# Attention and MLP on one core: tokens mapped 112 by 4, two heads scored as half-array matmuls, fixed buffers, a list-scheduled order

## The chip, the cores and the metric

One of the eight cores of a Trainium2 chip. The metric is device microseconds of one execution.

In the views, PE is TensorE, PEld its weight loads, DVE VectorE, ACT ScalarE, POOL GpSimd, and SP the queue that issues most of the DMA transfers.

## The reference

```python
# q, k, v: (8 batches, 12 heads, 448 tokens, 64); w_in: (768, 2048); w_out: (2048, 768); float32
q_n, k_n = rmsnorm(q, g_q), rmsnorm(k, g_k)          # over the 64 of a head
attn = softmax(q_n @ k_n.T / sqrt(64))               # per batch and head
x = (attn @ v) -> (8 * 448 tokens, 12 * 64 = 768)
h = x @ w_in
out = (h * clip(h + 3, 0, 6) / 6) @ w_out            # (3584, 768)
```

## The kernel before

It works on 48 head pairs (8 batches of 6). A pair's q and k are squared, reduced and scaled (normalisation), transposed on TensorE, multiplied to scores, exponentiated by ACT, and multiplied with v; a column of ones beside v gives the softmax sum. Matmuls of the MLP (`h` of the batch before, `y` of the batch before that) are merged between the attention steps by a fixed proportion. 448 tokens are 3 tiles of 128 and a rest of 64. The rests of two heads share one tile, which needs loads, squares, masks and transposes of its own.

A head has only 64 dimensions, and TensorE contracts 128 rows. The two heads of a pair lie above one another in the 128 rows, and a copy of k for each head is masked with zeros for the other head:

```python
kp = kp_pool.tile([128, 2, SM], BF16, name="kp")
for a in range(2):                       # masked copy of k for each head
    nc.vector.tensor_scalar_mul(kp[:, a, :], ps[:, 1]..., gmask[:, a:a + 1])
...
def score(P, u):                         # u = 0..6: 3 tiles x 2 heads, and the rest
    ...
    ps = ps_S.tile([128, S], FP32, name="s_ps")
    nc.tensor.matmul(out=ps[:], lhsT=lhsT, rhs=st["qT", b][:, j, :], start=True, stop=True)
    nc.scalar.activation(out=st["e", P][:, u, :], in_=ps[:], func=EXP, bias=zero_c[:], scale=1.0)
...
def att_items(P):                        # the order: loads 5 pairs ahead, prep 3, transposes 2
    items = [(0.0, lambda: load_step(P + 5)), (0.0, lambda: prep_step(P + 3)),
             (0.36, lambda: trans_step(P + 2))]
    ...
```

## Time and profile before

581.9 us (two runs, 581.15 and 582.66). Four parts of the profile's page follow: busy time of each engine; the span in 40 slices of 14.6 us, in tenths of busy time, with the granted TensorE clock; the chain of work that ended last; and two groups of instructions (busy us, mean ns of one, then idle time before them and who ended it).

```profile
PE 469.9 (81%) x3848; PEld 278.2 (48%) x3848; DVE 245.7 (42%) x544; ACT 320.5 (55%) x638; POOL 212.9 (37%) x245
...
PE   0045859877689888888788899888899999999996
...
PEclk9997998998999999979998999989999999999999
...
PE 35%; POOL 23%; DMA 19%; DVE 10%; ACT 5%; issue 4%; SPq 4%; POOLq 0%; ACTq 0%
DMA qk<-in_k_dram 15%; PE h_ps L356 14%; PE y_ps L373 13%; POOL qks L165 9%; POOL sq L138 9%; DVE ssq L159 4%; ACT t_sb L361 3%; PE s_ps L270 3%; SPq L190 2%; PE t_ps L248 2%; SPq L145 2%; POOL sqr L138 1%; DMA vr<-in_v_dram 1%; DMA qkr<-in_k_dram 1%; DVE xn L298 1%
...
L271 ACT ACTIVATE eT<-s_ps,zero_c 128x448 bf16<-128x448 f32 x336 | 200.9, 643 | 52.5 <-PE s_ps L270 50.0
...
L138 POOL TENSOR_TENSOR sq<-qk 128x768 f32<-128x768 f32 x45 | 66.0, 1468 | 88.4 <-DMA qk<-in_k_dram 80.6
```

TensorE is the busiest engine, but its slices are full only in the last third of the span. Nothing runs on it in the first two slices, and then they read between 4 and 9. The chain says why: it runs only 35% through TensorE, and 38% through the k loads (15%) and POOL (23%, most of it squaring and scaling), that is, through the preparation of the pairs.

Busy time overstates matmuls, because they overlap: one of 448 columns is listed with 360 ns, but the next starts 189 ns after it. For a sum one needs the time from one start to the next in back-to-back stretches, which I took from the trace: 448 columns 189 ns, 384 columns 162 ns, 512 columns 215 ns, 128 columns 56 ns. The next view is the timeline (start us, duration us, what, count, and in brackets the idle time before) of the first pair.

```profile
13.18 0.84 ACT L136 ACTIVATE sq<-qk 128x768 f32<-128x768 f32 x1 [8.63 <-DMA qk<-in_q_dram]
...
15.88 13.13 SPq L190 DMA_DIRECT2D vr<-in_v_dram  x4
32.71 0.84 ACT L136 ACTIVATE sqr<-qkr 128x768 f32<-128x768 f32 x1 [17.30 <-DMA vr<-in_v_dram]
...
34.72 0.50 PE L248 MATMUL t_ps<-identity,qks 128*128 128x128 bf16 x3 [34.72 <-POOL qks L165]
...
39.30 0.91 PE L270 MATMUL s_ps<-qT,kp 128*128 128x448 bf16 x2 [0.45 <-DVE qT L233]
```

The first pair's square is done at 14 us, but its transpose starts at 34.72 and its score at 39.30. In between, the second square of the rest tokens stands in ACT's queue ahead of everything else and waits until 32.71 for loads of small pieces.

| from the trace of before | us |
|---|---|
| span | 582.8 |
| until the first matmul | 34.7 |
| matmuls at their full-clock pace | 425.4 |
| extra while the clock was half | 13.1 |
| TensorE waiting: before 45 us, 45 to 100, after 100 | 5.2, 19.5, 80.1 |
| after the last matmul | 4.6 |

### The profile page before, as it was taken

How to read it: one execution, taken by the hardware profiler on the slowest of the kernel's cores; microseconds unless marked ns; L12 is line 12 of the kernel's file. 1: busy time of each engine (PE TensorE's matmuls, PEld its weight loads, DVE VectorE, ACT ScalarE, POOL GpSimd, SP SyncE). 2: the span in 40 equal slices, each digit the busy share in tenths (PEclk: the TensorE clock that was granted, in tenths of full speed). 3: DMA queues.
4: the chain of work that ended last, by engine and by line, in shares of the span. 5: the costliest groups of instructions: out<-in, count | busy, mean ns of one | idle time of the engine just before them, and what ended most of it. 6: DMA issues, size and time to landing. Idle time of an engine off the chain costs nothing.

```text
span 582.8 us, 9889 instructions
## 1 busy us (share of the span) xinstructions
PE 469.9 (81%) x3848; PEld 278.2 (48%) x3848; DVE 245.7 (42%) x544; ACT 320.5 (55%) x638; POOL 212.9 (37%) x245
## 2 busy tenths in 40 slices
PE   0045859877689888888788899888899999999996
PEld 0023535543345555544444455555455566654454
DVE  0035658864544453435543443544443434232200
ACT  1055977865566655636555666555667665733221
POOL 5069769974543532324434353223221100000000
PEclk9997998998999999979998999989999999999999
DMA  8974995462134222212222123222110000010012
GB/s 204 231 149 120 201 236 162 132 154 82 55 86 132 82 70 72 93 54 55 62 77 80 56 82 96 73 64 70 55 55 29 29 28 28 28 42 27 28 56 68
DMA packets 69648, 50.98 MB, mean 87 GB/s; under 512 B 22753, under 2 KB 68833, under 8 KB 69601
## 3 DMA queue, kind: packets, MB, share of 16 engines
q1 hardware_dynamic: 63168, 43.27, 26.4%
q0 software_dynamic: 2976, 6.29, 5.8%
q10 hardware_dynamic: 3456, 0.79, 0.7%
q8 instruction: 30, 0.49, 0.3%
q14 instruction: 18, 0.14, 0.1%
HBM read 45.61 MB, written 11.01 MB: 97 GB/s over the span
## 4 chain that ended last, share of the span: by engine, by line
PE 35%; POOL 23%; DMA 19%; DVE 10%; ACT 5%; issue 4%; SPq 4%; POOLq 0%; ACTq 0%
DMA qk<-in_k_dram 15%; PE h_ps L356 14%; PE y_ps L373 13%; POOL qks L165 9%; POOL sq L138 9%; DVE ssq L159 4%; ACT t_sb L361 3%; PE s_ps L270 3%; SPq L190 2%; PE t_ps L248 2%; SPq L145 2%; POOL sqr L138 1%; DMA vr<-in_v_dram 1%; DMA qkr<-in_k_dram 1%; DVE xn L298 1%
## 5 line engine op out<-in xcount | busy, mean ns | idle before, releaser
L271 ACT ACTIVATE eT<-s_ps,zero_c 128x448 bf16<-128x448 f32 x336 | 200.9, 643 | 52.5 <-PE s_ps L270 50.0
L361 ACT ACTIVATE t_sb<-h_ps,half_c 128x384 f32<-128x384 f32 (+1 forms) x128 | 81.1, 634 | 78.2 <-PE h_ps L356 78.0
L356 PEld LDWEIGHTS <-w_in_sb 128*128 128x128 bf16 x768 | 72.5, 98 | 95.5 <-issue 54.9
L165 POOL TENSOR_TENSOR qks<-qk,rs 128x384 bf16<-128x384 f32 x96 | 77.7, 831 | 103.4 <-PE t_ps L248 71.1
L270 PE MATMUL s_ps<-qT,kp 128*128 128x448 bf16 x288 | 97.1, 360 | 2.5 <-DVE kp L254 1.3
L138 POOL TENSOR_TENSOR sq<-qk 128x768 f32<-128x768 f32 x45 | 66.0, 1468 | 88.4 <-DMA qk<-in_k_dram 80.6
L159 DVE TENSOR_REDUCE ssq<-sq 128x12 f32<-128x768 f32 x48 | 45.7, 952 | 95.7 <-POOL sq L138 87.3
L279 PEld LDWEIGHTS <-eT 128*128 128x128 bf16 x1152 | 66.3, 100 | 30.4 <-issue 2.5
L248 PE MATMUL t_ps<-identity,qks 128*128 128x128 bf16 x288 | 26.1, 228 | 44.6 <-POOL qks L165 41.1
L379 ACT COPY y_sb<-y_ps 128x384 f32<-128x384 f32 x56 | 26.8, 479 | 44.0 <-PE y_ps L373 43.9
L248 PEld LDWEIGHTS <-qks 128*128 128x128 bf16 x288 | 20.9, 101 | 54.1 <-POOL qks L165 41.9
L130 ACT ACTIVATE rs<-ssq,eps_c 128x12 f32<-128x12 f32 x48 | 15.0, 313 | 51.9 <-POOL qks L165 37.3
L356 PE MATMUL h_ps<-xT_984,w_in_sb 128*128 128x512 bf16 x96 | 26.6, 394 | 11.3 <-DVE gT_1641 L363 10.7
L270 PEld LDWEIGHTS <-kp 128*128 128x128 bf16 x288 | 27.9, 99 | 16.3 <-DVE kp L254 1.7
L254 DVE TENSOR_SCALAR kp<-t_ps,gmask 128x384 bf16<-128x384 bf16 x96 | 35.2, 409 | 0.0
L356 PE MATMUL h_ps<-xT_2580,w_in_sb 128*128 128x512 bf16 x96 | 26.5, 389 | 6.9 <-DVE gT_3374 L363 6.7
L373 PE MATMUL y_ps<-w_out_sb,gT_1641 128*128 128x384 bf16 x128 | 28.0, 338 | 1.7 <-ACT y_sb L379 1.6
L373 PE MATMUL y_ps<-w_out_sb,gT_3374 128*128 128x384 bf16 x128 | 27.3, 332 | 1.7 <-ACT y_sb L379 1.6
L356 PE MATMUL h_ps<-xT_1757,w_in_sb 128*128 128x384 bf16 x96 | 22.0, 337 | 7.9 <-DVE gT_2459 L363 7.8
L250 DVE COPY qT<-t_ps 128x384 bf16<-128x384 bf16 x48 | 17.0, 355 | 26.6 <-PE t_ps L248 26.4
L298 DVE TENSOR_TENSOR xn<-x_ps,rd 128x384 bf16<-128x384 f32 x48 | 26.7, 555 | 1.2
L336 PE MATMUL xt_ps<-identity,xn 128*128 128x128 bf16 x144 | 17.3, 226 | 12.1 <-DVE xn L298 11.8
(104 smaller groups left out, 745.5 us busy)
## 6 DMA issues: line engine op xcount, KB each, us to landing
qk<-in_q_dram SPq DMA_DIRECT2D x48, 192.0 KB, 2.5
qk<-in_k_dram SPq DMA_DIRECT2D x48, 192.0 KB, 2.8
vf<-in_v_dram SPq DMA_DIRECT2D x48, 192.0 KB, 2.5
out_dram<-y_sb SPq DMA_DIRECT2D x48, 192.0 KB, 1.9
w_in_sb<-in_moe_w_in_dram POOLq DMA_DIRECT2D x6, 512.0 KB, 11.9
w_out_sb<-in_moe_w_out_dram POOLq DMA_DIRECT2D x4, 768.0 KB, 14.2
vr<-in_v_dram SPq DMA_DIRECT2D x16, 96.0 KB, 6.4
out_dram<-y_sb SPq DMA_DIRECT2D x16, 96.0 KB, 2.2
```

Source lines behind the costliest of these rows:

```text
L138: nc.gpsimd.tensor_tensor(out=out, in0=x, in1=x, op=A_MULT)
L159: nc.vector.tensor_reduce(out=ssq[:], in_=sq[:].rearrange("p (n d) -> p n d", d=D), axis=AX_X, op=A_ADD)
L165: nc.gpsimd.tensor_tensor(out=qks[:, i].rearrange("p t h d -> p h t d"), in0=qk[:, i].rearrange("p h (t d) -> p h t d", d=D), in1=rs4[:, i ...
L248: nc.tensor.transpose(ps[:, i, t, :], qks[:, i, t].rearrange("p h d -> p (h d)"), identity[:])
L254: nc.vector.tensor_scalar_mul(kp[:, a, :], ps[:, 1].rearrange("p t c -> p (t c)"), gmask[:, a:a + 1])
L270: nc.tensor.matmul(out=ps[:], lhsT=lhsT, rhs=st["qT", b][:, j, :], start=True, stop=True)
L271: nc.scalar.activation(out=st["e", P][:, u, :], in_=ps[:], func=EXP, bias=zero_c[:], scale=1.0)
L279: nc.tensor.matmul(out=dst[:, a * E1:(a + 1) * E1], lhsT=eT[:, u, c0:c0 + 128], rhs=va[:, a, t, :], start=(first and a == 0 and t == 0), s ...
L298: nc.vector.tensor_tensor(out=xn[:], in0=xv[:, :, :, 0:D], in1=rd[:].unsqueeze(3).to_broadcast([128, NT, 2, D]), op=A_MULT)
L356: nc.tensor.matmul(out=h_ps[:, 0:n], lhsT=w_in_sb[:, kt, f * 128:(f + 1) * 128], rhs=st["xT", G][:, kt, :], start=(kt == 0), stop=(kt == N ...
L361: nc.scalar.activation(out=t_sb[:, 0:n], in_=h_ps[:, 0:n], func=RELU, bias=half_c[:], scale=1.0 / 6.0)
L373: nc.tensor.matmul(out=y_ps, lhsT=gT[:, f, i * 128:(i + 1) * 128], rhs=w_out_sb[:, f, nh * HALF:(nh + 1) * HALF], start=(f == 0), stop=(f ...
```

## The change

The intent: no rest tokens (448 = 4 tiles of 112), no masked copies (each head's scores contract 64 rows, one head in the upper and one in the lower half of the array, so that both matmuls can run at once), one `exp` over both heads, and an order found by a list schedule: before the kernel is built, a program simulates the engines with a fixed cost for each step and gives the engine that comes free next its most urgent ready step. The file is nearly rewritten; its core:

```diff
-    ps_S = pool("ps_S", 3, space=PSUM)                 # 3 score buffers, one bank each
+    S_r = [psum.tile([128, 2, 512], FP32, name=f"S{i}") for i in range(2)]  # 2, two banks each
@@ scores
-        ps = ps_S.tile([128, S], FP32, name="s_ps")
-        nc.tensor.matmul(out=ps[:], lhsT=lhsT, rhs=st["qT", b][:, j, :], start=True, stop=True)
-        nc.scalar.activation(out=st["e", P][:, u, :], in_=ps[:], func=EXP, bias=zero_c[:], ...)
+            for a in range(2):
+                r = slice(a * 64, a * 64 + 64)
+                em(nc.tensor.matmul(
+                    out=ps[:, a, 0:S], lhsT=kT[r, t * TP:t * TP + 128], rhs=qT[r, :],
+                    start=True, stop=True))
+            em(nc.scalar.activation(
+                out=eT[:, t], in_=ps[0:TP, :, 0:S], func=EXP, bias=0.0, scale=1.0))
+        plan.add(PE, 0.25, 0.42, want, f_s, ...)       # 0.25 us of TensorE in the schedule
@@ preparation
+        early = P < 3                                   # squares on ACT, else on POOL
+            eng = DVE if P == 0 or (P < 8 and i == 0) else POOL   # scaling of q, of k
@@ order
-        for _, fn in merge(att, mlp):
-            fn()
+    for i in plan.order():                              # greedy, over simulated engines
+        plan.ops[i][4]()
```

Matmuls per pair change from 7 transposes, 7 scores of 448 columns, 28 value products and 3.5 transposes back to 8, 8 (half array), 32 and 4. The MLP's columns are the same. `em` ties each instruction to the one before it on its engine, so the planned order is the executed order.

## The prediction

> **What bounds the kernel now.** TensorE. In back-to-back stretches of the timeline a 448-column matmul starts every 189 ns, 384 columns every 162, 512 every 215, 128 every 56, 65 every 33. With the counts of the groups view that is: scores 336 x 189 = 63.5 us, values 1152 x 33 + 192 x 56 = 49, transposes 504 x 56 = 28, h 145, y 145: 430 us of matmul work in a 583 us span. The remaining 150 us are: 34.7 us before the first transpose (timeline: the 256-byte rest-token loads hold the DMA queues, and the rest squares sit ahead of everything in order on ACT and POOL); about 113 us of stalls after it; 4.5 us of last copy and store. The windows view puts the stalls early: PE busy 0.68 at 40 to 60 us, about 0.8 from 130 to 300, 0.97 from 400 on. The chain of waits names loads of k (15%), POOL scaling and squares (18%): input preparation, not ACT (55% busy).
>
> **What the change does, costed.**
> 1. No rest tokens: their small loads (24 us of full-DMA time, summed packet times), squares, masks and transposes go. First transpose at 11 to 13 us: q and k land at about 8, then half square 0.6, reduction 0.7, two small ACTIVATEs 0.6, scaling 0.7. Gain about 23 us.
> 2. Scores: 4 pairs of K=64 matmuls instead of 7 of K=128 per head pair. The Trainium skill ("TensorE: Matmul & The Clock Gate", Packing small matmuls) says different row groups run concurrently, starts about 4 ns apart; "TensorEngine Tiling (Array Packing)", Key Properties, says that changing tiling mode drains the engine. No run here shows either. Estimate: 189 ns plus about 60 for two switches, 192 x 0.25 = 48 us against 63.5. If they ran serially: 73 us.
> 3. Values 1536 x 33 = 51, transposes 384 x 49 + 192 x 56 = 30, h 768 x 189 = 145, y 145: unchanged within 3 us. Total matmul work about 419 us.
> 4. ACT: 192 exps of 896 columns without bias pointer, about 0.91 us each (0.643 + 448 x 0.83 ns - 0.10, the difference of copy and relu at 384), 175 us against 201. Off the path, except during the first six pairs, where ACT at about 4 us per pair sets the pace and PE has only 2.6 us of work.
> 5. POOL about 4.7 us per pair (square 1.95, two scalings 1.1, cast 0.6), under the 8 to 9 us a pair takes: no limit. DVE about unchanged.
> 6. List order plus early loads: most of the preparation stalls go.
>
> **Sum.** First scores 12; pairs of batch 0 until about 36 (ACT-bound); batch 1 with h of batch 0 until about 71; then 370 us of matmul work; 4.5 tail: 446 at no stall. With 5% stalls (two PSUM buffers for h and y, one for values; h groups back to back need about 1.5 us against 1.13 of matmuls) and some half-clock windows: **468 us**, range 450 to 498. Faster by over 2%: 0.97; within: 0.02; slower: 0.01.
>
> **What would show it.** First PE work near 12 us; score matmuls of a pair starting within 10 ns and about 0.25 us to the next group; exp near 0.91 us; PE busy over 0.9 from 80 us on; chain dominated by PE h and y, POOL and k loads under 10% together; ACT about 290 us busy.
>
> **What would make it wrong.** Each tiling-mode switch draining fully (0.17 us each, twice per group: +50 us); serial halves (+25); the fixed order fitting the chip badly so that waits on the single value buffer, two score buffers or h evacuations cost over 10% (+25); weights landing late.

## The result

500.0 us (two runs, 499.02 and 500.98), ratio 0.8587, 95% interval 0.8534 to 0.8640. That is 2 us outside the range (450 to 498) and 32 us above the predicted 468. All ratios here are those of a kernel's runs to the runs of the kernel before in the same rounds, so not quite the ratio of the medians quoted. The same lines of the page, after:

```profile
PE 461.8 (93%) x4160; PEld 264.9 (53%) x4160; DVE 234.5 (47%) x432; ACT 295.1 (59%) x485; POOL 213.6 (43%) x204
...
PE   1688999899998999899999999999999999989996
...
PEclk9999899999999999999999999999999999999999
...
PE 81%; DMA 7%; DVE 3%; ACT 3%; issue 2%; POOL 2%; SPq 1%; POOLq 0%; ACTq 0%; DVEq 0%
PE M L397 30%; PE M L364 26%; PE S L303 9%; PE X L320 9%; DMA qk<-in_k_dram 6%; PE S L283 3%; PE X L342 2%; ACT eT L308 2%; DMA qk<-in_q_dram 1%; DVE gT L375 1%; ACT ts L372 1%; POOL qks L253 1%; DVE xn L335 1%; SPq L201 1%; DVE ssq L227 0%
...
L308 ACT ACTIVATE eT<-S 112x896 bf16<-112x896 f32 x192 | 171.8, 916 | 61.4 <-PE S L303 59.9
...
L224 POOL TENSOR_TENSOR sq<-qk 112x1024 f32<-112x1024 f32 x45 | 84.8, 1894 | 9.9 <-DMA qk<-in_k_dram 4.0
```

TensorE's slices read 8 or 9 from the third on, the last one apart, the chain now runs 81% through TensorE, and the score products L303 are 9% of it. POOL and loads together are 9%, as predicted. One `exp` takes 916 ns for 896 columns, against 643 ns for 448 before. The score groups themselves are seen in the timeline of TensorE alone:

```profile
199.38 0.81 PE L397 MATMUL M<-w_out_sb,gT 128*128 128x384 bf16 x4
200.12 0.36 PE L303 MATMUL S<-qT,kT 64*128 64x448 bf16 x2
200.42 0.82 PE L397 MATMUL M<-w_out_sb,gT 128*128 128x384 bf16 x4
```

Four y matmuls of 162 ns from 199.38 would be over at 200.03, but the score pair starts at 200.12. A pair of 448 columns in parallel would be over 189 ns later, at 200.31, but the next y matmul starts at 200.42. In all 192 groups the two halves start at most 6 ns apart, mostly 3: they do run at once. Over the whole trace, the matmul before a group takes 96 ns longer than its pace to the group's start (285 instead of 189 after 448 columns, 258 instead of 162 after 384), and the group takes 292 ns to the next matmul instead of 189. So a group costs 96 + 3 + 292 = 391 ns; two full-array matmuls would take 378. Not in the 391 ns: the first full-array matmul after a group takes 10 to 11 ns more than its pace to the next one (173 instead of 162 after 384 columns, 200 instead of 189 after 448). These 2 us stand among the waits of the next table.

The sum of the trace:

| us | before | after | difference |
|---|---|---|---|
| span | 582.8 | 497.3 | -85.5 |
| until the first matmul | 34.7 | 6.5 | -28.2 |
| matmuls at their full-clock pace | 425.4 | 401.0 | -24.4 |
| entering and leaving the half-array mode | 0 | 34.3 | +34.3 |
| extra while the clock was half | 13.1 | 10.9 | -2.2 |
| waiting before 45 us | 5.2 | 13.5 | +8.3 |
| waiting 45 to 100 us | 19.5 | 6.9 | -12.6 |
| waiting after 100 us | 80.1 | 19.1 | -61.0 |
| after the last matmul | 4.6 | 4.8 | +0.2 |

The 34.3 us are counted with at most 96 ns per entry and 103 ns per exit, 173 of each (19 groups stand directly behind another group). The change gains by the early start and by the vanished waits. What it saves in matmuls it pays back in switches. "Entering" and "leaving" name where the two gaps stand, before and after a group; the run with 112 columns shows below that most of the gap after the group is the group's own weight load.

### The profile page after: what moved, and what is told of

Its sections match the earlier page's. It is cut to its first block, busy times and chain, and to the rows that moved or that the text cites. A ratio compares the mean times of both kernels' runs of the same rounds, so it can differ in the third digit from the quotient of the medians. Undisturbed runs are those within 1.5% of the kernel's fastest.

```text
span 497.3 us, 10192 instructions
## 1 busy us (share of the span) xinstructions
PE 461.8 (93%) x4160; PEld 264.9 (53%) x4160; DVE 234.5 (47%) x432; ACT 295.1 (59%) x485; POOL 213.6 (43%) x204
## 4 chain that ended last, share of the span: by engine, by line
PE 81%; DMA 7%; DVE 3%; ACT 3%; issue 2%; POOL 2%; SPq 1%; POOLq 0%; ACTq 0%; DVEq 0%
PE M L397 30%; PE M L364 26%; PE S L303 9%; PE X L320 9%; DMA qk<-in_k_dram 6%; PE S L283 3%; PE X L342 2%; ACT eT L308 2%; DMA qk<-in_q_dram 1%; DVE gT L375 1%; ACT ts L372 1%; POOL qks L253 1%; DVE xn L335 1%; SPq L201 1%; DVE ssq L227 0%
## 5 line engine op out<-in xcount | busy, mean ns | idle before, releaser
L308 ACT ACTIVATE eT<-S 112x896 bf16<-112x896 f32 x192 | 171.8, 916 | 61.4 <-PE S L303 59.9
L364 PE MATMUL M<-xT,w_in_sb 128*128 128x448 bf16 x768 | 171.0, 354 | 4.1 <-DVE gT L375 3.8
L397 PE MATMUL M<-w_out_sb,gT 128*128 128x384 bf16 x896 | 160.2, 326 | 0.5 <-DVE gT L375 0.5
L253 POOL TENSOR_TENSOR qks<-qk,rs 112x512 bf16<-112x512 f32 x87 | 91.8, 1076 | 118.4 <-PE S L283 86.8
L375 DVE SCALAR_TENSOR_TENSOR gT<-ts,M 128x448 bf16<-128x448 f32 x128 | 78.5, 618 | 105.3 <-ACT ts L372 104.6
L372 ACT ACTIVATE ts<-M,half_c 128x448 f32<-128x448 f32 x128 | 80.5, 636 | 59.5 <-PE M L364 57.3
L397 PEld LDWEIGHTS <-gT 128*128 128x128 bf16 x896 | 82.3, 98 | 60.3 <-issue 11.1
L224 POOL TENSOR_TENSOR sq<-qk 112x1024 f32<-112x1024 f32 x45 | 84.8, 1894 | 9.9 <-DMA qk<-in_k_dram 4.0
L303 PE MATMUL S<-qT,kT 64*128 64x448 bf16 x384 | 72.5, 380 | 5.7 <-DVE kT L291 3.0
L320 PE MATMUL X<-va,eT 112*128 112x65 bf16 x1536 | 72.8, 199 | 1.9 <-ACT eT L308 1.2
L283 PE MATMUL S<-identity,qks 112*128 112x112 bf16 x384 | 32.4, 223 | 15.9 <-DVE qks L253 12.4
L303 PEld LDWEIGHTS <-kT 64*128 64x128 bf16 x384 | 19.0, 94 | 36.7 <-issue 27.9
L346 DVE COPY xT<-X 128x448 bf16<-128x448 bf16 x48 | 18.7, 389 | 31.1 <-PE X L342 30.8
L289 DVE COPY qT<-S 128x448 bf16<-128x448 bf16 x48 | 18.7, 389 | 28.2 <-PE S L283 17.3
L291 DVE TENSOR_SCALAR kT<-S,gp_t 128x448 bf16<-128x448 bf16 x48 | 21.4, 445 | 18.2 <-PE S L283 18.2
## 6 DMA issues: line engine op xcount, KB each, us to landing
w_out_sb<-in_moe_w_out_dram POOLq DMA_DIRECT2D x4, 768.0 KB, 10.9
```

The lines of the kernel that those rows point to most:

```text
L224: em(nc.gpsimd.tensor_tensor(out=o, in0=x, in1=x, op=A_MULT))
L253: em((nc.vector if eng is DVE else nc.gpsimd).tensor_tensor(out=qks[:, i].rearrange("p t h d -> p h t d"), in0=qk[:, i].rearrange("p h (t ...
L283: em(nc.tensor.transpose(ps[:, t * TP:(t + 1) * TP], qks[:, i, t].rearrange("p h d -> p (h d)"), identity[0:TP, 0:TP]))
L303: em(nc.tensor.matmul(out=ps[:, a, 0:S], lhsT=kT[r, t * TP:t * TP + 128], rhs=qT[r, :], start=True, stop=True))
L308: em(nc.scalar.activation(out=eT[:, t], in_=ps[0:TP, :, 0:S], func=EXP, bias=0.0, scale=1.0))
L320: em(nc.tensor.matmul(out=X_ps[:, a, i * E1:(i + 1) * E1], lhsT=eT[:, t, a, C0[i]:C0[i] + 128], rhs=va[:, a, t, :], start=(t == 0 and i == ...
```

## The experiments

Theory A: the miss is mainly the price of entering and leaving the half-array mode. Rivals: the halves are worth what was predicted and the waits are at fault (B); the wrong cost in the schedule spoils the order (C); a half-array matmul is slow in itself (D). Changes are against the changed kernel; where nothing else is said, its order is kept.

### Full-array scores instead of half-array ones

```diff
-                    em(nc.vector.tensor_scalar(dst[:, 0:S], ps[:, 0:S], gp_t[:], 8.0, A_MULT, A_MULT))
+                    for a in range(2):     # two masked copies of k, as in the kernel before
+                        em(nc.vector.tensor_scalar_mul(dst[:, a, 0:S], ps[:, 0:S], gm_t[:, a:a + 1]))
-                    out=ps[:, a, 0:S], lhsT=kT[r, t * TP:t * TP + 128], rhs=qT[r, :],
+                    out=ps[:, a, 0:S], lhsT=kT[:, a, t * TP:t * TP + 128], rhs=qT[:, :],
```

> Scores as two full-array matmuls (K=128) from two masked copies of k instead of two half-array ones; same order of instructions. Theory A (the half-array pair is fast, 192 ns, but entering and leaving it costs 96 + 103 ns): a full-array group takes 2 x 189 = 378 ns against 391, no gap around it; total within 1% of the changed kernel, 493 to 503 us, perhaps 2 us better. Rival B (the miss lies in stalls and the fixed order, the halves are worth what the prediction said, 250 ns a group): 192 x (378 - 250) = 25 us slower, about 525 us. VectorE gets 21 us more work in both.

Measured: 500.79 us, ratio 0.8593 (0.8572 to 0.8615), the same as the change, not the 2 us better that A held possible. B expected 525 and falls. TensorE's timeline around a score group in this run:

```profile
199.34 0.81 PE L398 MATMUL M<-w_out_sb,gT 128*128 128x384 bf16 x4
199.99 0.54 PE L304 MATMUL S<-qT,kT 128*128 128x448 bf16 x2
200.36 1.30 PE L398 MATMUL M<-w_out_sb,gT 128*128 128x384 bf16 x7
```

The group starts at 199.34 + 4 x 0.162 = 199.99, with no gap, and the next matmul 0.37 us later. In the sum, matmuls rise by 35.4 us and the 34.3 us of switches vanish; the half-clock loss is some 5 us smaller (full clock from 30.8 us on) and the waits some 6 us larger. The half-array scoring, looked at alone, is worth nothing in this kernel.

### The schedule's cost of a score group corrected

```diff
-        plan.add(PE, 0.25, 0.42, want, f_s, ...)
+        plan.add(PE, 0.39, 0.56, want, f_s, ...)
```

> Only the schedule's cost of a score group is set to what the trace shows (0.39 us of TensorE instead of 0.25). Theory A: the switches are paid anyway; the better order gains at most part of the 17 us of stalls after 100 us: 492 to 502 us. Rival C (the schedule's wrong cost is what spoils the order and costs most of the miss): 475 to 485 us.

Measured: 501.92 us, ratio 0.8612 (0.8591 to 0.8634). C falls: with the right cost the waits are no smaller (42.5 us in all against 39.5).

### Two score groups per entry

```diff
-        for t in range(2):
-            score(P, t, w + t * step)      # one group of two matmuls, one buffer
+        score(P, 0, w)                     # two groups, four matmuls, both buffers; then two exps
-        plan.add(PE, 0.25, 0.42, want, f_s, ..., [("S", u, 0), ("S", u, 1)])
+        plan.add(PE, 0.58, 0.75, want, f_s, ..., [("S", u, a) for u in us for a in range(2)])
```

> Two score groups back to back per entry into the half-array mode (96 entries instead of 192), both score buffers filled at once, costs in the schedule as measured. Theory A: each pair of groups takes about 96 + 200 + 292 = 588 ns against 2 x 391 = 782, so 96 x 0.19 = 18 to 19 us less TensorE time, less some new waits on the two buffers: 478 to 488 us. Rival D (a half-array matmul itself costs more, whatever stands beside it): no gain, 495 to 505 us or worse.

Measured: 517.0 us, ratio 0.8893 (0.8830 to 0.8956): slower and far outside A's range. By its total alone D ("or worse") would stand; the trace decides. Its timeline:

```profile
178.27 1.14 PE L400 MATMUL M<-w_out_sb,gT 128*128 128x384 bf16 x6
179.34 0.55 PE L304 MATMUL S<-qT,kT 64*128 64x448 bf16 x4
179.82 0.99 PE L400 MATMUL M<-w_out_sb,gT 128*128 128x384 bf16 x5
```

The four matmuls take 0.48 us to the next one, where two separate groups would take two times 0.29 and be entered twice. In groups that stand directly behind one another, the third matmul starts 199 ns after the first. So theory A's arithmetic holds: there are 96 entries instead of 173, and the switches fall from 34.3 to 18.2 us. But the waits rise from 39.5 to 63.5 us and the half-clock loss from 10.9 to 19.4 us: its records show half clock in four later stretches instead of one (that the larger gaps let the clock fall is likely, but not tested). Each double group needs both score buffers empty at the same moment. This run has another order than the change, so I cannot say how much of the new waiting comes from the buffers and how much from the order.

### Each score pair computed twice

```diff
-            for a in range(2):
+            for a in (0, 1, 0, 1):
```

> Each score pair is computed twice in a row, same result, no further switch. Theory A: 192 x 0.20 = 38 us more, about 538 us, a little less where TensorE was waiting. Rival D (half-array matmuls themselves cost 391 ns a pair): 192 x 0.39 = 75 us more, about 575 us.

Measured: 525.13 us, ratio 0.9006 (0.8975 to 0.9038). D (575 us) falls. The trace has 37.1 us more matmul time, which is 193 ns for each extra pair, as A says, and almost the same switch cost (32.8 us). The total rose by only 25 us because the half-clock loss fell by 6.4 us (full clock from 25.2 us on instead of 42.7) and the waits by 4.7 us. The extra work of the first 45 us delayed nothing: 21 exps were done by then against 20. That is a first hint on the early part, taken up below.

### A dummy half-array matmul after each group of four y matmuls, and its full-array control

```diff
                            start=(f == 0), stop=(f == NFT - 1)))
+                    em(nc.tensor.matmul(         # control: identity[:, :] and identity[:, 0:16]
+                        out=ps[:, 448:464], lhsT=identity[0:64, :], rhs=identity[0:64, 0:16],
+                        start=True, stop=True, skip_group_check=True))
```

> One half-array matmul of 16 columns, into unread PSUM columns, after each of the 224 groups of four y matmuls. Theory A (the price belongs to entering and leaving the half-array mode, not to scores): a gap of about 96 ns before and 103 ns after each, about 0.2 us times 224 = 45 to 50 us more, 540 to 550 us. Rival E (the gaps belong to the score matmuls, their operands or their two banks): about 25 ns each, 503 to 508 us.

> Control of the dummy: the same 16 columns as a full-array matmul. Both theories: no gap, about 27 ns each, 224 x 0.027 = 6 us more, 503 to 509 us.

Measured in one look each: 542.61 us with half-array dummies, 501.12 us with full-array ones. Both give a wrong result: a matmul with the start flag in the same bank breaks off the accumulation of y. The Trainium skill says so ("PSUM — Partial Sum Buffer", The four PSUM rules: the flag clears the accumulation bits of the whole bank), and the error of these runs agrees: it is 0.864 in both, and if only the last 4 of the 16 products of each sum survive, I estimate the square root of 12/16, or 0.87. Both runs have the same fault and the same number of instructions, so their times can be compared. The control came out 2 us below its expected range. The timeline of TensorE with half-array dummies (L401 is the dummy, L397 the y matmuls):

```profile
159.36 0.18 PE L401 MATMUL M<-identity 64*128 64x16 bf16 x1
159.47 0.82 PE L397 MATMUL M<-w_out_sb,gT 128*128 128x384 bf16 x4
160.23 0.18 PE L401 MATMUL M<-identity 64*128 64x16 bf16 x1
160.34 0.82 PE L397 MATMUL M<-w_out_sb,gT 128*128 128x384 bf16 x4
```

And the same view with full-array dummies:

```profile
154.41 0.17 PE L401 MATMUL M<-identity 128*128 128x16 bf16 x1
154.44 0.81 PE L397 MATMUL M<-w_out_sb,gT 128*128 128x384 bf16 x4
155.09 0.17 PE L401 MATMUL M<-identity 128*128 128x16 bf16 x1
155.12 0.81 PE L397 MATMUL M<-w_out_sb,gT 128*128 128x384 bf16 x4
```

Four y matmuls and a dummy take 0.87 us with the half array and 0.68 with the full one. The matmul before a half-array dummy takes 258 ns instead of 162 (entry: 96), and the dummy 112 instead of 28 (exit: 84). That is 180 ns times 224 = 40.3 us, and the times differ by 41.5 us, one run against one. So the price belongs to the switch, whatever is computed in it. Rival E falls.

### 112 weight columns

```diff
-                    out=ps[:, a, 0:S], lhsT=kT[r, t * TP:t * TP + 128], rhs=qT[r, :],
+                    out=ps[0:TP, a, 0:S], lhsT=kT[r, t * TP:t * TP + TP], rhs=qT[r, :],
```

> Half-array scores with 112 weight columns instead of 128. If the gap at the entry is the weight load that is not hidden (96 ns beside a load of 92 to 98 ns), it changes with the load's recorded duration; if it is a fixed drain, it stays at 96 ns whatever the load takes. Total 495 to 505 us unless the load becomes much longer.

Measured in one look: 505.39 us, just above the expected range. The recorded weight load of a half grew from 92 to 123 ns. The entry stayed (93 ns instead of 96), and the exit grew from 103 to 137 ns. So neither half of the expectation is right as it stands: the load's length is in the gap after the group, nearly one for one (31 ns more load, 34 ns more gap), and not in the gap before it. The weight loads in the trace of the change say the same:

```profile
199.35 0.46 PEld L397 LDWEIGHTS <-gT 128*128 128x128 bf16 x4
200.12 0.10 PEld L303 LDWEIGHTS <-kT 64*128 64x128 bf16 x2 [0.32 <-issue]
200.41 0.60 PEld L397 LDWEIGHTS <-gT 128*128 128x128 bf16 x5 [0.20 <-issue]
```

A full-array matmul has its load start a whole matmul earlier (161 ns ahead, in the median, for 384 columns), but the load of a half starts only 4 ns ahead of its matmul, and its 92 ns are then still to come. So at a switch the weight load is not hidden behind the matmul before, as it is elsewhere. What the 96 ns before it are, these runs do not settle.

### The list schedule undone

```diff
-    for i in plan.order():
+    for i in order:        # by wanted time alone (weights by their earliest time), dependencies kept
```

> The list schedule undone: instructions in the order of the wanted times alone, no simulated engines. Theory A with the prediction's step 6 (the order is what removed the stalls): stalls after 100 us rise from 17 us to 30 to 70 us, 515 to 560 us. Rival F (the fixed buffers and the missing rest tokens removed them, the order is worth little): 495 to 510 us.

Measured: 795.04 us, ratio 1.364 (1.359 to 1.369), far beyond my expectation. Waits in its trace (us in total, times, longest):

```profile
POOL qks L253 <- ACT rs L236: 482.2, 45, 15.5
DVE gT L375 <- ACT ts L372: 274.5, 118, 8.3
ACT eT L308 <- PE S L303: 227.7, 156, 3.9
```

POOL's scaling waits 482 us, and the last it waits for is ACT. But ACT is not what holds it. One pair's way from the square to the scaling shows where the time goes:

```profile
300.83 1.89 POOL L224 TENSOR_TENSOR sq<-qk 112x1024 f32<-112x1024 f32 x1
...
310.07 1.21 DVE L227 TENSOR_REDUCE ssq<-sq 112x16 f32<-112x1024 f32 x1
...
314.22 0.31 ACT L232 ACTIVATE rs<-ssq,eps_c 112x16 f32<-112x16 f32 x1
...
314.86 2.04 POOL L253 TENSOR_TENSOR qks<-qk,rs 112x512 bf16<-112x512 f32 x2 [12.13 <-ACT rs L236]
```

Between square and reduction the trace has 386 us in all (median 7.8), between reduction and ACT's step only 16 us. So it is VectorE's queue that holds the preparation, behind steps such as gT that wait for ACT and TensorE themselves. Rival F falls: with the same fixed buffers and no rest tokens, but in this order, the kernel is much slower than the old one. But this order is no neutral one, so the run does not measure how much of the 61 us of vanished late waits the list schedule alone removed.

### What sets the pace of the first 70 us

The prediction had 12 pairs done by 71 us. The trace has 33 of 48 exps (8 pairs) and 60 of 96 h matmuls by then. In the first 42.7 us TensorE runs at half speed: 65-column value products start every 54 ns, later every 29. Theory G: the half clock costs its time in full. Theory I: the loads of q, k and v wait behind the weights (the chain of waits holds one k load of 12.35 us). Theory J: POOL. The counts of exps and h matmuls here and below are taken from the traces. The windows view of the change follows; its columns are the stretch, its length, then busy us and instructions of TensorE, its weight loads, VectorE, ACT and POOL, then granted clock, DMA share and GB/s:

```profile
12.00:36.00 24.00, 19.32 (x174) 11.28 (x173) 16.23 (x27) 13.90 (x25) 21.70 (x18) 1.00 1.17 250
36.00:45.00 9.00, 7.85 (x69) 4.26 (x67) 5.43 (x11) 6.67 (x11) 5.12 (x7) 1.00 1.16 263
45.00:71.00 26.00, 23.45 (x245) 13.31 (x244) 16.16 (x30) 18.22 (x31) 18.04 (x17) 0.93 1.11 238
```

POOL is busy 21.70 of 24 us, and the DMA engines are full as well (share 1.17). ACT, which I had predicted to set the pace, is busy only 13.90. The clock column reads 1.00 although TensorE runs at half speed there: the trace's clock records begin with a rise at 42.7 us, and the time ahead of them is counted as full.

Useless matmuls in TensorE's empty time at the start:

```diff
+        if plan.ops[i][0] == PE:     # 36 before the first step, 40 before the third
+            more = 36 if seen == 0 else 40 if seen == 2 else 0
+            for _ in range(more):
+                em(nc.tensor.matmul(out=M_r[0][:, 0:128], lhsT=identity[:], rhs=identity[:],
+                                    start=True, stop=True))
```

> 76 matmuls without use (128 columns, into an unused buffer) in the empty TensorE time before the second pair's transposes (36 before the first transposes, 40 after them). Theory G (up to 42.7 us the granted clock is half, and that costs about 11 us: 65 columns every 54 ns instead of 29): if the clock rises early and stays, up to 11 us less, 488 to 496 us; if it falls again in the gaps that follow, no change, 498 to 502 us. Rival H (TensorE's speed before 43 us does not matter, the inputs do): 498 to 502 us although values then start every 29 ns.

> As the warm start, with 60 instead of 40 useless matmuls after the first transposes and 6 ahead of each of the next 42 TensorE steps (0.3 us each at full clock), so that the clock stays up. Theory G: full clock from about 10 us on, gain of the 11 us less what the fillers delay: 488 to 498 us. Rival H: 500 to 506 us, no gain although values start every 29 ns.

> Full-array scores with the filled warm start. Theory A and G: as the filled warm start within 3 us (the full array needs 378 ns a group, the halves 391): 486 to 498 us.

Measured: warm start 496.68 us, ratio 0.8512 (0.8468 to 0.8556), between its two expected ranges; filled 502.69, 0.8609 (0.8551 to 0.8667); filled with full-array scores 502.01, 0.8611 (0.8560 to 0.8662): within 3 us of the filled one, as expected, but like it above theory G's range. The warm start had full clock from 7.1 us and lost it again at 13.9; its interval overlaps that of the change. The filled one kept full clock from 7.4 to 325 us, and had 12 exps done by 36 us and 19 by 45, where the change has 13 and 20. But its fillers took all the idle time themselves (19.7 us of them), so it cannot tell G from H. Hence a lighter one, 2 fillers per step:

> The filled warm start with 2 useless matmuls per step instead of 6, a third of the delay. If the clock stays full: theory G (the half clock costs its 11 us in full) 489 to 494 us and more than 20 exps by 45 us; rival H (TensorE is not what the first 45 us wait for) 494 to 500 us with 19 to 21 exps by 45 us. If the clock falls again this run says nothing new over the warm start.

Measured: 497.81 us, ratio 0.8545 (0.8511 to 0.8579), 19 exps by 45 us. The clock was full from 6.2 to 16.4 and from 30.1 us on, and half between, so this is not the clean test that it was meant to be. With half the clock loss of the change on its own matmuls (5.7 us against 10.9) the pairs came no earlier. Together with the doubled scores this speaks for H: early on TensorE is not what is waited for. A small cost of the clock is not excluded: the two warm starts lie 3.3 and 2.2 us below the change, with overlapping intervals.

Weights 8 us later, and the squares of pairs 3 to 7 on ACT:

```diff
-    weights(10.0, 36.0)
+    weights(18.0, 44.0)
```

```diff
-        early = P < 3
-        parts = [(0,), (1,)] if early else [(0, 1)]
+        early = P < 8
+        parts = [(0,), (1,)] if P < 3 else [(0, 1)]
```

> Both weight transfers wanted 8 us later. Theory I (early on the loads of q, k, v wait behind the weights: one k load took 12.4 us from issue to landing): the first pairs come earlier, 3 to 8 us less, 491 to 497 us. Rival G (the half clock, not the inputs, slows the first 43 us): 498 to 506 us.

> The squares of pairs 3 to 7 go from POOL (1.9 us each) to ACT, as those of pairs 0 to 2 already do. Theory J (POOL, 90% busy from 12 to 36 us, sets the pace of the first pairs): about 9 us less POOL work early, more than the 20 exps done by 45 us (23 or more), 492 to 497 us. Rival K (something else sets it): 19 to 21 exps by 45 us, 498 to 503 us.

Measured: weights late 497.59 us, ratio 0.8518 (0.8476 to 0.8559), which lies between the ranges of I and G, with 19 exps by 45 us; not separable from the change. Squares on ACT: **491.08 us**, ratio 0.8420 (0.8392 to 0.8447), a little better than the expected range, with 25 exps by 45 us instead of 20, and 81 h matmuls by 71 us instead of 60. The windows view of that run, with the same columns:

```profile
12.00:36.00 24.00, 20.18 (x216) 11.64 (x216) 17.64 (x31) 21.67 (x34) 13.16 (x16) 1.00 1.17 248
36.00:45.00 9.00, 7.22 (x108) 4.49 (x107) 6.90 (x14) 8.14 (x13) 5.94 (x7) 1.00 1.16 259
45.00:71.00 26.00, 25.31 (x248) 14.22 (x248) 18.50 (x35) 20.17 (x36) 21.25 (x20) 1.00 1.14 249
```

POOL falls from 21.70 to 13.16 us between 12 and 36, ACT rises from 13.90 to 21.67, and the pairs come faster, with the same DMA share of 1.17. The clock is a rival here, as full clock began at 26.3 us instead of 42.7. But the doubled scores had it from 25.2 us on and only 21 exps by 45 us, so the clock alone does not bring the 25. This supports theory J, that POOL set the pace; the move also changes the schedule's order, which this run does not keep apart. Do the causes add?

> Squares of pairs 3 to 7 on ACT and the weights 8 us later. If both causes are real and separate, their gains add: 488 to 495 us; if they are the same wait, no better than the better of the two alone: 494 to 499 us.

> The same with the warm start of 76 useless matmuls. 485 to 493 us if the half clock also costs on its own; otherwise within 2 us of the kernel without the warm start.

Measured: with late weights 492.69 us (0.8450, 0.8422 to 0.8479), with the warm start as well 493.64 us (0.8468, 0.8445 to 0.8492). They do not add: 492.69 us lies in the range that was expected for adding gains, but it is no better than the squares on ACT alone. That kernel is the best, 1.9% below the change (under 2%, but with intervals that do not overlap) and 15.8% below the kernel before (both by the ratios).

## Why the prediction was wrong

What was right, with the trace's number: first scores at 12.3 us (12 predicted); exp 916 ns (0.91 us; the 0.83 ns a column in it is the cost in the schedule's own table, and the traces give (916 - 643 + 104) / 448 = 0.84); ACT 295 us busy (about 290); TensorE above 0.9 from 80 us on; POOL and loads 9% of the chain (under 10%); most preparation stalls gone (80.1 to 19.1 us after 100 us); halves starting within 10 ns (6 at most). First work on TensorE came earlier than predicted (6.5 us instead of about 12). What made it wrong was named in advance as well: mode switches that cost more.

1. **The term "189 ns plus about 60 for two switches" failed.** Two switches cost 199 ns. I had taken the size from the schedule's own 0.25 us and not from a measurement; the page gave the drain no number. That is 34.3 us instead of 192 x 0.06 = 11.5, so 22.8 us of the miss. The full-array run, the doubled scores and the dummies show it.
2. **Values were overestimated.** The slot of 33 ns read from the kernel before is 29 ns here, 1536 times: about 6 us the other way, which by luck hid part of the miss.
3. **"POOL ... no limit" and "ACT-bound" failed for the first pairs.** I compared POOL's 4.7 us per pair with the steady 8 to 9 us, not with the 4 us at which I let the first pairs come. Idle and half-clock time together were 57 us (6.5 + 10.9 + 39.5) where the prediction's sum leaves 468 - 419 - 4.5 = 44.5. These 12 to 13 us are the rest of the miss. Half to three quarters of them come back when five squares leave POOL (6 us between the two traces, 9 us between the medians; in the traces half of it is less half-clock loss and half fewer waits).

The three give 22.8 - 6 + 12.4 = 29 us, which is the span of 497.3 less the predicted 468. This is bookkeeping and no further proof, as the third term is what the trace has left over. A timed run lies about 2 us above its own span (499.02 against 497.3 here), as it does in the other runs.

## What to carry to other kernels

Two concurrent half-array matmuls save time only if enough of them stand together to pay for the way in and out: here one pair of 448 columns saved 186 ns and paid 199, or about 210 with the slower matmul after it. Before believing a packed matmul, look in the trace at the matmul before it and the one after it, not at the pair itself, and check that the buffers allow larger groups. A rate that is harmless in the steady state (POOL's 4.7 us per pair) can set the pace of a start-up in which the pairs are wanted every 4 us (supported here by one move of work that also changed the order), so cost the start-up on its own.

## What the Trainium skill lacked or had wrong

- "TensorEngine Tiling (Array Packing)", Key Properties, says that a change of tiling mode drains the engine. A gap at each switch agrees in kind, but the page gives no cost. These runs show 96 ns before and 103 ns after a pair of 448 columns, 96 and 84 ns around a 16-column dummy. Inside the mode the next pair starts after 199 ns.
- "TensorE: Matmul & The Clock Gate", Packing small matmuls, has starts about 4 ns apart, and the trace agrees (mostly 3, at most 6 ns). Its span model has no term for the weight load at a switch, which is not hidden here: the load of a half starts 4 ns ahead of its matmul, and a load of 123 instead of 92 ns made the gap after the group 34 ns longer.
- The same page, The HAM clock gate, gives a busy window after which the clock rises, but not how busy is enough. Here TensorE was busy 19.32 of 24 us from 12 to 36 us (in the profile's sense) at half clock; 76 dense useless matmuls raised the clock at 7.1 us, and it fell at 13.9. In the five runs with such a start full clock came at 6.2 to 8.1 us, in all others at 25 us or later.
- None of the pages that I read says that the profile's granted clock counts the time before the first clock record as full: it read 1.00 for 12 to 36 us while 65-column matmuls started every 54 ns instead of 29.
